# Last sixteen rows of the tenth K tile through Pool's DMA queue, w_mod in two loads (adaLN block with cached attention, decode step, one core)

## The chip, the cores and the metric

The kernel is one program on one core of one Trainium2 chip. A core has five engines with instruction streams of their own: TensorE (PE in the profile, its weight loads PEld), VectorE (DVE), ScalarE (ACT), GpSimd (POOL) and SyncE (SP), which here only issues transfers. Sixteen DMA engines move data between HBM and the core's SBUF, whose rows are 128 partitions; in this document they are called lanes, to keep them apart from the five. A transfer is issued by an instruction of SP, ACT or Pool, and each of these three has a queue of its own on the lanes. The metric is the device time of one execution in microseconds; the value for a kernel is the median of several runs.

## What is computed

One decode step of a transformer block for 8 sequences, all in float32: an adaptive layer norm from a condition `c`, attention of one new token over the last 2048 positions of a cache (32 query heads, 8 key and value heads, head size 128), a projection, a residual, a second adaptive layer norm and a feed-forward part with a squared ReLU.

```
mod = (silu(c) @ w_mod).reshape(8, 6, 1, 512)          # sa, ca, ga, sb, cb, gb
h = layernorm(x) * (1 + ca) + sa
q = (h @ wq) as 32 heads of 128
k, v = the last 2048 positions of k_cache, v_cache (8 heads, each used by 4 query heads)
o = softmax(q k^T / sqrt(128)) v
x = x + ga * (o @ wo)                                   # wo: 4096 x 512
h = layernorm(x) * (1 + cb) + sb
x = x + gb * (relu(h @ w1 + b1)^2 @ w2 + b2)            # 512 -> 1792 -> 512
```

Nearly all of the bytes are K and V: 8 heads x 8 sequences x 2048 positions x 128 numbers of 4 bytes is 67 MB each. With the weights the core reads 165 MB once, and each K and V number is used for four query heads only.

## The kernel before, in words

**Tiles.** K comes in 16 tiles, K0 to K15, and V in 16, each of 4 MB: for one key head, four of the eight sequences. A tile fills 128 partitions with 32 KB each. For K, partition 4p + u holds 64 consecutive positions of sequence u of the four, so the rows of the tile follow p, and within p the sequence u. The weights are w_mod (6 MB, 48 KB a partition), wq (8 MB), wo (four parts of 2 MB), w1 and w2.

**Slots.** SBUF holds four places of 4 MB ("big") and one of 2 MB ("small"), here all cut out of one tile called `home` (L80 to L85), so that w_mod, which takes a big and the small place side by side, is one transfer (L124), and wq, which takes two bigs, is one too (L128). The list `loads` (L144 to L149) fixes the order of all transfers: w_mod, wq, K0, K1, then alternately a K and a V tile with the parts of wo between them, and at the end the last V tiles, the last part of wo, w1 and w2. `pump` (L152) issues the next transfer of the list as soon as a place of its size is free, and `done` (L157) frees a place when its last reader has been written down. All of these are issued by SP and wait in SP's queue for the work that frees the place.

**Work.** DVE transposes each K tile in eight pieces (L190), PE makes the scores (L359), the softmax for a head runs over both its K tiles (L369 to L433, with ACT's exponentials), PE multiplies with V (L446) and projects with wo (L486). The order of the instructions on each engine is written out by hand in the loop over `s`; V work runs five steps (`PV_LAG`) behind. When the last wo product is done the second layer norm and the feed-forward part follow (L568 to L640). w2 is loaded in five pieces, the last two of one row group each (L136), and the multiplication with w2 (L630) follows the pieces as they land. The result leaves with one transfer (L640).

**The start.** The inputs `x` and `c` come, already laid out by the host, as `xc`: rows on four groups of 8 partitions (0 to 7, 32 to 39, 64 to 71, 96 to 103). ACT issues them in six transfers (L68): the first two carry x and c together, the rest one each. ACT's exponential for silu(c) (L201) waits for them, then follow DVE's statistics, PE's multiplication with w_mod (L278) and with wq (L304), and only then can scores begin.

**Pool** fills a few constants at the start, one more tile near the end (L502), and issues no transfer.

**Semaphores.** The transfers of SP and ACT share eight semaphores in rotation, in program order; one that takes a semaphore again waits for the transfer that had it before.

Of the kernel before, what the change touches and what calls it, by code (L numbers as in the profile page):

```python
# [8 lines left out]
F32 = mybir.dt.float32  # L9
# [4 lines left out]
EPS = 1e-5  # L14
BIG_SLOTS = 4
PV_LAG = 5


@with_exitstack
def tile_adaln_cached_attention_mlp(  # L20
# [14 lines left out]
    nc = tc.nc  # L35
    P = 128
    B, HKV, SK, DH = k_cache.shape
    D = wq.shape[0]
# [14 lines left out]
    consts = ctx.enter_context(tc.tile_pool(name="consts", bufs=1))  # L53
# [10 lines left out]
    nc.vector.memset(xc_in, 0.0)  # L64
    for q in range(D // P):
        b = slice(32 * q, 32 * q + B)
        for x, y in ((0, 2),) if q < 2 else ((0, 1), (1, 2)):
            nc.scalar.dma_start(xc_in[b, x:y], xc[b, x:y])  # L68

    ident = consts.tile([P, P], F32, name="ident")  # L70
# [6 lines left out]


    big = NJ * DH
    home = consts.tile([P, BIG_SLOTS * big + big // 2], F32, name="home")  # L80
    base = [2 * big, 0, big, 3 * big + big // 2]
    slots = {
        "big": [home[:, o : o + big] for o in base],
        "small": [home[:, 3 * big : 3 * big + big // 2]],
    }  # L85
    free = {size: list(range(len(ts))) for size, ts in slots.items()}
    held = {}

    def size_of(key):
        return "small" if key[0] in ("wo", "w1") or key == ("mod", 1) else "big"  # L90

    def load(key):
        kind, i = key
        held[key] = free[size_of(key)].pop(0)
        if kind in ("mod", "wq") and i == 0:
            return
        t = slots[size_of(key)][held[key]]
        if kind in "KV":

            hk, c = divmod(i, 2)  # L100
            v = k_cache[4 * c : 4 * c + 4, hk] if kind == "K" else v_cache[c::2, hk]
            v = v[:, SK - W :, :].rearrange("u (p j) d -> p u (j d)", j=NJ)
            cuts = (0, big // 2, big * 3 // 4, big) if key == ("V", 2 * HKV - 1) else (0, big)
            for x, y in zip(cuts, cuts[1:]):
                nc.sync.dma_start(t[:, x:y], v[..., x:y])
            return

        def rows(o, v):
            n = v.shape[1] * v.shape[2]
            nc.sync.dma_start(t[:, o : o + n].rearrange("p (a n) -> p a n", n=v.shape[2]), v)  # L110

        w1v = w1.rearrange("(p kc) n -> p kc n", p=P)

        def wo_rows(j):

            r = 2 * REP * DH
            return wo[j * r : (j + 1) * r, :].rearrange("(h p i) n -> p h (i n)", p=P, i=4)

        if kind == "wo":
            rows(0, wo_rows(i))  # L120
        elif kind == "mod":

            o = base[held["mod", 0]]
            nc.sync.dma_start(home[:, o : o + big + big // 2], w_mod.rearrange("(p kc) n -> p (kc n)", p=P))  # L124
        elif kind == "wq":

            o = base[held["wq", 0]]
            nc.sync.dma_start(home[:, o : o + 2 * big], wq.rearrange("(p k) n -> p (k n)", p=P))  # L128
        elif kind == "tail":
            rows(0, wo_rows(HKV // 2 - 1))  # L130
            rows(big // 2, w1v[:, 0:2])
        elif kind == "w1":
            rows(0, w1v[:, 2:4])
        else:
            v = w2.rearrange("(p c) n -> p c n", p=P)
            for lo, hi in ((0, 8), (8, 10), (10, 12), (12, 13), (13, 14)):  # L136
                rows(D * lo, v[:, lo:hi])
# [14 lines left out]
    def pump():  # L152
        while at[0] < len(loads) and free[size_of(loads[at[0]])]:
            load(loads[at[0]])
            at[0] += 1
# [86 lines left out]
    for k in (2, 3, 4):  # L242
        n = 1 << k
# [27 lines left out]
    for i, last in enumerate((16, 8)):  # L271
        at_ = 0
        while at_ < last:
            kc, m = divmod(16 * i + at_, 6)
            n = min(4 - m if m < 4 else 6 - m, last - at_)
# [233 lines left out]

    for s in range(N + PV_LAG + 1):  # L510
        g, i = divmod(s, C)
        q, h = divmod(s, 2)
        v = s - PV_LAG
        soft = 1 <= g <= HKV
# [122 lines left out]
    y = work.tile([P, P], F32, name="y", tag="one_y", bufs=1)  # L637
# [39 lines left out]
```

## Time and profile before

| | |
|---|---|
| median of 3 runs | 394.15 us (393.83 to 394.23) |
| profiled execution | 393.95 us |
| its span, first to last instruction | 392.2 us |
| PE busy | 251.7 us (64%) |
| DVE busy | 219.6 us (56%) |
| ACT busy | 46.1 us (12%) |
| Pool busy | 1.3 us (0%) |
| read from HBM | 164.67 MB, 420 GB/s over the span |
| SP's queue (q1) | 7424 packets, 98.2% of the lanes' time |

The span runs from the first to the last instruction; the profiled execution's own time is 1.75 us more. A busy share of the lanes is the time that packets took, over 16 lanes. A packet on SP's queue is one row of a transfer in one partition, 32 KB for a K or V tile, or the 4 bytes with which a lane tells that its share of a transfer has landed. In the chain of work that ended last, "DMA home<-..." is time in which that chain waited for a transfer to land. The queue called "instruction" carries the programs of the engines themselves, fetched in blocks while the kernel runs.

### The profile page before, as it was taken

What the parts mean: (1) busy time and instruction counts of PE and PEld (TensorE: products, weight loads), DVE (VectorE), ACT (ScalarE), POOL (GpSimd) and SP (SyncE); (2) the same over time, 40 slices, a digit from 0 to 9 for tenths busy, and PEclk for the clock granted to TensorE, in tenths of its full rate; (3) what the DMA queues carried; (4) which work ended last, traced back from release to release, by engine and by line L of the source; (5) the groups of instructions that cost most, each with busy time, mean ns of one, the idle gap of its engine ahead of it and who ended that gap; (6) DMA issues with size and microseconds to landing.
All of it is one profiled execution on the core that took longest, in us unless ns stands there. A gap on an engine that the chain in (4) does not pass through costs nothing.

```text
span 392.2 us, 4671 instructions
## 1 busy us (share of the span) xinstructions
PE 251.7 (64%) x2006; PEld 77.0 (20%) x2006; DVE 219.6 (56%) x315; ACT 46.1 (12%) x89; POOL 1.3 (0%) x8
## 2 busy tenths in 40 slices
PE   0006859779328873897384828882874838896796
PEld 0002211012102221222121202220221202233333
DVE  1006479998057735783582817881676358755231
ACT  0012021131003100310031002010111003004010
POOL 0000000000000000000000000000000000000000
PEclk9999989999959995999598797998697969998999
DMA  8999999999999999999999999999999999999994
GB/s 327 444 442 431 434 431 431 428 426 404 450 428 431 426 431 431 423 436 445 429 423 434 434 429 428 428 429 428 409 445 431 433 431 434 428 418 419 426 421 177
DMA packets 7557, 165.04 MB, mean 421 GB/s; under 512 B 824, under 2 KB 1008, under 8 KB 1520
## 3 DMA queue, kind: packets, MB, share of 16 engines
q1 hardware_dynamic: 7424, 164.70, 98.2%
q8 instruction: 16, 0.26, 0.3%
q10 hardware_dynamic: 112, 0.04, 0.0%
q14 instruction: 5, 0.04, 0.0%
HBM read 164.67 MB, written 0.07 MB: 420 GB/s over the span
## 4 chain that ended last, share of the span: by engine, by line
DMA 61%; DVE 20%; PE 14%; issue 3%; ACT 1%; ACTq 0%; POOL 0%; DVEq 0%; POOLq 0%; SPq 0%
DMA home<-in_A_k_cache_dram 44%; DVE kT L190 12%; PE s_ps L359 7%; DMA xc_in<-in_xc_dram 6%; DMA home<-in_B_w_dram 6%; DMA home<-in_A_v_cache_dram 5%; PE o_ps L446 2%; PE m_ps L304 2%; DVE pT L425 2%; PE p_ps L390 1%; DVE pr L418 1%; DVE qbd L322 1%; DVE o_sb L464 1%; DVE mx L373 0%; DVE qst L268 0%
## 5 line engine op out<-in xcount | busy, mean ns | idle before, releaser
L190 DVE STREAM_TRANSPOSE kT<-home 128x1024 f32<-128x1024 f32 x128 | 151.2, 1219 | 83.8 <-DMA home<-in_A_k_cache_dram 79.6
L359 PE MATMUL s_ps<-kT,qst 128*32 128x512 f32 x512 | 129.2, 1076 | 20.5 <-DVE kT L190 19.5
L446 PE MATMUL o_ps<-home,pT 128*32 128x256 f32 x1024 | 70.0, 397 | 10.6 <-DVE pT L425 9.7
L446 PEld LDWEIGHTS o_ps<-home,pT 128*32 128x32 f32 x1024 | 33.9, 117 | 101.4 <-issue 62.4
L375 PE MATMUL m_ps<-ident,mx 128*1 128x128 f32 x16 | 4.3, 365 | 58.8 <-DVE mx L373 58.8
L359 PEld LDWEIGHTS s_ps<-kT,qst 128*32 128x32 f32 x512 | 14.4, 115 | 40.4 <-DVE kT L190 32.0
L224 PE MATMUL m_ps<-xsum,sel 128*128 128x1 f32 x2 | 0.6, 362 | 32.5 <-DVE xsum L222 32.5
L425 DVE STREAM_TRANSPOSE pT<-pr 128x2048 f32<-128x2048 f32 x8 | 18.2, 2274 | 1.0 <-ACT pr L408 1.0
L408 ACT ACTIVATE pr<-pr,own 128x512 f32<-128x512 f32 x16 | 17.8, 1220 | 0.3
L402 ACT ACTIVATE pr<-p_ps,nm 128x512 f32<-128x512 f32 x8 | 5.5, 688 | 96.8 <-DVE nm L399 96.8
L347 ACT COPY qst<-q_ps 32x128 f32<-32x128 f32 x32 | 8.2, 256 | 70.2 <-PE q_ps L336 70.0
L369 ACT COPY ss<-s_ps 128x512 f32<-128x512 f32 x8 | 4.7, 585 | 98.9 <-issue 69.9
L202 DVE TENSOR_SCALAR e_sb<-e_sb 128x128 f32<-128x128 f32 x1 | 0.2, 226 | 27.2 <-ACT e_sb L201 27.2
L375 PEld LDWEIGHTS m_ps<-ident,mx 128*1 128x1 f32 x16 | 0.7, 81 | 64.0 <-DVE mx L373 64.0
L390 PE MATMUL p_ps<-ss,perm 128*128 128x512 f32 x16 | 12.1, 844 | 0.0
L399 DVE TENSOR_SCALAR nm<-m_ps 128x1 f32<-128x1 f32 x8 | 1.3, 159 | 16.8 <-PE m_ps L395 16.8
L418 DVE TENSOR_SCALAR pr<-pr,own 128x512 f32<-128x512 f32 x16 | 9.2, 656 | 0.8 <-ACT pr L402 0.8
L486 PE MATMUL wo_ps<-home,oT 128*32 128x512 f32 x64 | 8.3, 600 | 1.8 <-DMA home<-in_A_wo_dram 1.8
L463 DVE TENSOR_SCALAR o_sb<-o_ps,bit 128x128 f32<-128x128 f32 x16 | 4.9, 306 | 6.1 <-PE o_ps L446 6.1
L429 PE MATMUL m_ps<-zs,tsel 128*128 128x8 f32 x16 | 2.9, 252 | 8.1 <-DVE zs L420 8.1
L304 PE MATMUL m_ps<-home,h1T 128*32 128x512 f32 x64 | 7.1, 594 | 1.5 <-DVE add L294 1.5
L278 PE MATMUL m_ps<-home,cT 128*32 128x512 f32 (+1 forms) x64 | 7.6, 642 | 0.0
(118 smaller groups left out, 115.5 us busy)
## 6 DMA issues: line engine op xcount, KB each, us to landing
home<-in_A_k_cache_dram SPq DMA_DIRECT2D x16, 4096.0 KB, 23.9
home<-in_A_v_cache_dram SPq DMA_DIRECT2D x15, 4096.0 KB, 20.3
home<-in_A_wo_dram SPq DMA_DIRECT2D x4, 2048.0 KB, 25.7
home<-in_w_mod_dram SPq DMA_DIRECT2D x1, 6144.0 KB, 17.4
home<-in_B_w_dram SPq DMA_DIRECT2D x2, 1792.0 KB, 28.5
home<-in_A_v_cache_dram SPq DMA_DIRECT2D x1, 2048.0 KB
home<-in_A_v_cache_dram SPq DMA_DIRECT2D x2, 1024.0 KB
home<-in_B_w_dram SPq DMA_DIRECT2D x1, 2048.0 KB
```

What stands on the lines that cost most here:

```text
L190: nc.vector.transpose(KTS[q, j][:, rows], k[:, rows, 32 * j : 32 * j + 32])
L278: nc.tensor.matmul(pms[m // 4][32 * q : 32 * q + 32, m % 4 * P : (m % 4 + n) * P].rearrange("p (m n) -> p m n", n=P), cT[:, kc, :], wv[:, ...
L304: nc.tensor.matmul(pqs[r][32 * g : 32 * g + 32, :], hT[:, kc, :], w[:, 4 * r + g, :], start=(kc == 0), stop=(kc == NQ - 1),)
L347: nc.scalar.copy(own[b, :, :, i, 0], pq[b, :P].rearrange("p (c m t) -> p c m t", c=2, t=REP))
L359: nc.tensor.matmul(s_ps[0][32 * g : 32 * g + 32, :], qst[hk % 2][:, P * (4 * c + u) + 32 * j :][:, :32], kT[:, u], start=(c == 0 and j == ...
L390: nc.tensor.matmul(sp, perm, SS_.pop(hk), start=True, stop=True)
L402: nc.scalar.activation(pr.rearrange("p j x -> p (j x)"), SS_.pop(hk), AF.Exp, bias=nm, scale=SCALE, accum_out=z)
L408: nc.scalar.mul(X_[hk][..., w], pr, own[:, w : w + 1])
L418: nc.vector.tensor_scalar(X_[hk][..., w], pr, own[:, w : w + 1], None, op0=ALU.mult)
L425: nc.vector.transpose(PT_[hk].rearrange("p e j r -> p j e r"), X_.pop(hk).rearrange("p j x w -> p j (x w)"))
L446: nc.tensor.matmul(O_[n][32 * g : 32 * g + 32, : 2 * DH], PT_[hk][:, e, j : j + 2].rearrange("p j r -> p (j r)"), vt[:, j : j + 2, :].rear ...
L486: nc.tensor.matmul(wo_ps[32 * i : 32 * i + 32, :], oT[hk % 2][:, i, :], w[:, 4 * (hk % 2) + i, :], start=(hk == 0), stop=(hk == HKV - 1),)
```

## The change

The sixteen rows p = 16 to 31 of sequence u = 3 of the tile K9 (partitions 67, 71, ... 127) are loaded by Pool's queue, in six transfers of 3, 2, 4, 3, 2 and 2 rows. Between them stand five transfers of 4, 6, 4, 5 and 6 single numbers of b1 into a tile `step` that nothing reads. The table `WALK` lists all eleven, with 1 for rows and 0 for unread numbers. The other 112 rows of K9 come in four transfers of SP's queue, one for each sequence u: 32, 32, 32 and 16 rows, each going to every fourth partition.

With it, `home` loses the 2 MB place, which becomes a tile `small` of its own, and the big places change order. w_mod comes in two transfers, 32 KB a partition to a big place and 16 KB a partition to `small`. `xc` comes in eight transfers instead of six, each with x or c alone. The first and the third part of wo come in two transfers each. In all, SP and ACT issue eight transfers more: two for xc, one for w_mod, two for wo and three for K9. No computing instruction is added, removed or moved on any engine.

```diff
--- before.py
+++ after.py
@@ -14,6 +14,7 @@
 EPS = 1e-5
 BIG_SLOTS = 4
 PV_LAG = 5
+WALK = ((3, 1), (4, 0), (2, 1), (6, 0), (4, 1), (4, 0), (3, 1), (5, 0), (2, 1), (6, 0), (2, 1))
 
 
 @with_exitstack
@@ -64,7 +65,7 @@
     nc.vector.memset(xc_in, 0.0)
     for q in range(D // P):
         b = slice(32 * q, 32 * q + B)
-        for x, y in ((0, 2),) if q < 2 else ((0, 1), (1, 2)):
+        for x, y in ((0, 1), (1, 2)):
             nc.scalar.dma_start(xc_in[b, x:y], xc[b, x:y])
 
     ident = consts.tile([P, P], F32, name="ident")
@@ -77,12 +78,13 @@
 
 
     big = NJ * DH
-    home = consts.tile([P, BIG_SLOTS * big + big // 2], F32, name="home")
-    base = [2 * big, 0, big, 3 * big + big // 2]
+    home = consts.tile([P, BIG_SLOTS * big], F32, name="home")
+    base = [3 * big, 0, big, 2 * big]
     slots = {
         "big": [home[:, o : o + big] for o in base],
-        "small": [home[:, 3 * big : 3 * big + big // 2]],
+        "small": [consts.tile([P, big // 2], F32, name="small")],
     }
+    step = consts.tile([8, len(WALK)], F32, name="step")
     free = {size: list(range(len(ts))) for size, ts in slots.items()}
     held = {}
 
@@ -92,7 +94,7 @@
     def load(key):
         kind, i = key
         held[key] = free[size_of(key)].pop(0)
-        if kind in ("mod", "wq") and i == 0:
+        if key == ("wq", 0):
             return
         t = slots[size_of(key)][held[key]]
         if kind in "KV":
@@ -100,6 +102,20 @@
             hk, c = divmod(i, 2)
             v = k_cache[4 * c : 4 * c + 4, hk] if kind == "K" else v_cache[c::2, hk]
             v = v[:, SK - W :, :].rearrange("u (p j) d -> p u (j d)", j=NJ)
+            if key == ("K", 9):
+
+                d = t.rearrange("(p u) n -> u p n", u=4)
+                for u in range(4):
+                    n = 32 if u < 3 else 16
+                    nc.sync.dma_start(d[u][:n], v[:n, u])
+                for j, (m, real) in enumerate(WALK):
+                    if real:
+                        nc.gpsimd.dma_start(d[3][n : n + m], v[n : n + m, 3])
+                        n += m
+                    else:
+                        nc.gpsimd.dma_start(step[:m, j : j + 1], b1[:m].rearrange("(a n) -> a n", n=1))
+                assert n == 32
+                return
             cuts = (0, big // 2, big * 3 // 4, big) if key == ("V", 2 * HKV - 1) else (0, big)
             for x, y in zip(cuts, cuts[1:]):
                 nc.sync.dma_start(t[:, x:y], v[..., x:y])
@@ -117,11 +133,13 @@
             return wo[j * r : (j + 1) * r, :].rearrange("(h p i) n -> p h (i n)", p=P, i=4)
 
         if kind == "wo":
-            rows(0, wo_rows(i))
+            cuts = (0, 2) if i == 1 else (0, 1, 2)
+            for x, y in zip(cuts, cuts[1:]):
+                rows(4 * D * x, wo_rows(i)[:, x:y])
         elif kind == "mod":
 
-            o = base[held["mod", 0]]
-            nc.sync.dma_start(home[:, o : o + big + big // 2], w_mod.rearrange("(p kc) n -> p (kc n)", p=P))
+            v = w_mod.rearrange("(p kc) n -> p (kc n)", p=P)
+            nc.sync.dma_start(t, v[:, big:] if i else v[:, :big])
         elif kind == "wq":
 
             o = base[held["wq", 0]]
```

## The prediction

> **What bounds the kernel now.** I read the page's header and DMA part first, then the chain of waits, then stretches of time with the lanes' busy share, and last the waits of single engines.
>
> ```profile
> span 392.2 us, 4671 instructions
> ...
> DMA  8999999999999999999999999999999999999994
> ...
> q1 hardware_dynamic: 7424, 164.70, 98.2%
> q8 instruction: 16, 0.26, 0.3%
> ```
>
> ```profile
> 20.00:380.00 360.00, 242.92 (x1874) 72.39 (x1876) 216.11 (x300) 46.01 (x89) 0.47 (x1) 0.90 1.00 428
> 385.00:385.50 0.50, 0.50 (x20) 0.50 (x24) 0.00 (x0) 0.00 (x0) 0.00 (x0) 1.00 0.70 270
> 385.50:386.00 0.50, 0.50 (x29) 0.50 (x22) 0.00 (x0) 0.00 (x0) 0.00 (x0) 1.00 0.62 250
> 386.00:386.50 0.50, 0.50 (x28) 0.50 (x22) 0.00 (x0) 0.00 (x0) 0.00 (x0) 1.00 0.48 193
> 386.50:387.00 0.50, 0.50 (x28) 0.50 (x24) 0.00 (x0) 0.00 (x0) 0.00 (x0) 1.00 0.49 188
> 387.00:387.50 0.50, 0.49 (x19) 0.22 (x12) 0.00 (x0) 0.00 (x0) 0.00 (x0) 1.00 0.52 201
> 387.50:388.00 0.50, 0.50 (x16) 0.26 (x14) 0.00 (x0) 0.00 (x0) 0.00 (x0) 1.00 0.36 135
> 388.00:388.50 0.50, 0.45 (x12) 0.16 (x8) 0.00 (x0) 0.00 (x0) 0.00 (x0) 1.00 0.01 4
> ```
>
> ```profile
> 344.99 21.49 DMA home<-in_A_v_cache_dram
> 366.54 22.08 DMA home<-in_B_w_dram
> 388.62 0.04 issue
> 388.67 0.47 PE m_ps L630 x8
> 389.16 0.30 DVE y L638
> 389.48 0.29 DVE y L639
> ```
>
> The last two columns of a stretch are the lanes' busy share and GB/s. From 20 to 380 us the share is 1.00: no lane runs dry, and 428 GB/s over 16 lanes is 26.75 GB/s each, so a 32 KB row takes 1.22 us and a 4 MB tile 9.8 us. The chain ends on the landing of w2's last rows; after it come only eight matmuls, two DVE steps and the output. So the time is the end of the latest lane plus a fixed tail. The lanes do not end together: the share falls to 0.5 by 386 and stays there until 388. Summed over the six stretches from 385 to 388, what is missing to 1.00 is 1.4 us; that, with 0.1 to 0.2 us after 388, is the most that a perfect balance of the lanes could save.
>
> The packet records (start, length, queue, size) show which lanes. On a lane a packet starts 3 to 5 ns before the last one ends, so the records can be strung into sixteen lanes of 464 packets of SP's queue each:
>
> ```
> end of last w2 row, us                            program blocks that the lane fetched before
> 384.95 384.95 385.05 385.16 385.17                none
> 385.38 385.69 385.99                              one
> 387.67 387.71 387.77 387.86 387.88 387.93 388.08  two of 16 KB
> 388.16                                            three of 8 KB
> ```
>
> A 16 KB block takes 1.06 us and makes the row behind it 0.47 us longer: 1.5 us, twice on the same seven lanes. This imbalance is what moving rows can work on.
>
> **The change: the small edits.**
>
> ```profile
> 1.18 0.42 SPq L128 DMA_DIRECT2D home<-in_A_wq_dram  x1
> ...
> 27.88 1.28 ACT L201 ACT_TABLE_LOAD   x1 [27.88 <-DMA xc_in<-in_xc_dram]
> ...
> 34.42 7.57 PE L278 MATMUL m_ps<-home,cT 128*32 128x512 f32 x64
> ```
>
> ```profile
> home<-in_A_wq_dram SPq DMA_DIRECT2D x1, 36.4
> ```
>
> ```profile
> 43.48 7.08 PE m_ps L304 x64
> ...
> 54.29 2.43 DVE kT L190 x3
> ```
>
> xc lands at 27.9 because each of its packets takes turns with a 48 or 64 KB row of SP's queue. With w_mod's rows of 32 and 16 KB the sixteen turns of eight xc transfers (one for the row, one for its completion) fit into w_mod's time, so xc lands near 18 us (estimate). L278 moves with it; L304 can start when wq lands, 1.2 + 36.4 = 37.6 instead of 43.5, and the transposes up to 6 us sooner. It is worth nothing: the share is 1.00, so the first K tiles are no bound of the end. The other way, w_mod's second transfer waits for the first xc transfer (it reuses the next semaphore). The first eight rows last until about 1.8 + 8 x 1.22 = 11.6 us; xc's first must land before about 10, and with shorter rows to wait for it should at 7. If not, the lanes idle for the difference; I take 0, bound 1.2 us, one row. Splitting wo, and all other added transfers, costs completion packets: 8 + 11 transfers at 9 ns are 0.17 us a lane at most; I take 0.1. Since eight transfers of SP and ACT are added, the rotation of eight semaphores stands as before from the last wo on.
>
> **The change: issuing K9.**
>
> ```profile
> 180.13 0.54 SPq L105 DMA_DIRECT2D home<-in_A_k_cache_dram  x1
> 200.66 0.53 SPq L105 DMA_DIRECT2D home<-in_A_v_cache_dram  x1
> 206.62 0.54 SPq L105 DMA_DIRECT2D home<-in_A_k_cache_dram  x1
> 223.09 0.54 SPq L105 DMA_DIRECT2D home<-in_A_v_cache_dram  x1
> 225.27 0.54 SPq L105 DMA_DIRECT2D home<-in_A_k_cache_dram  x1
> ```
>
> ```profile
> 214.49 6.88 DVE L190 STREAM_TRANSPOSE kT<-home 128x1024 f32<-128x1024 f32 x6 [7.27 <-DMA home<-in_A_k_cache_dram]
> ```
>
> ```profile
> POOL pr L502 <- DVE pT L425: 357.1, 1, 357.1
> ```
>
> ```profile
> out_dram<-y SPq DMA_DIRECT2D x1, 64.0 KB, 1.5
> ```
>
> K9 is issued at 180.1 and read at 214.5. SP's three more issues cost 3 x 0.54 = 1.6 us; behind them stands V7, which goes out at 200.7 anyway. Pool has nothing to do until 358 us. Its issue is not in the trace: between 0.54 us as on SP and 0.54 + 1.5 with a whole landing after each, eleven take 6 to 22 us, inside the 34 us. If that cover were gone, DVE would start K9 late and K11 (225.3) be issued late; ahead of K11 in the queue are then V7, K10 and V8, so some 18 us are left before a lane runs dry. I take 0.
>
> **The change: which lane carries which row.** As WALK reads, with a cursor that starts at lane 0 and goes on by one lane per row or number, three lanes get 10 rows of K9 (0, 7, 8), three get 9 (1, 2, 15), one 8 and nine 7, instead of 8 each. If each row kept its 1.22 us and the +2 lanes were ones that end at 385.0, they would end at 387.4 and the late ones at 386.9: 0.7 us less than 388.1.
>
> But the rows also change partitions. In every load of before that has 128 partitions, all rows take the same time, whatever the tile. The few small loads show what a foreign write does. Four rows of b1 and b2 go to partitions 0 to 3 on four lanes, and xc's last two transfers to 96 to 103 on eight:
>
> ```
> lane        what it carries   rows of SP's queue, ns (usual 311 / 2418)
> one of b's  own w rows        422, 335, 361 right after b1 and b2
> one         own wq rows       2467 and 2512, at xc's last two
> another     own wq rows       2447 and 2501, at the same
> ```
>
> Only these three lanes are slowed, by 199, 142 and 112 ns. The foreign bytes, at 26.75 B/ns, are 3 x (1792 + 512) = 258 ns for the first and 2 x 2048 = 153 ns for each of the others, so the lane that owns a stripe of partitions loses some 0.8 of the time of foreign bytes. The four earlier xc transfers slowed nobody, so it isn't a law.
>
> The Trainium skill has the rule ("SBUF — State Buffer", section on door 1, the DMA port swizzle): sixteen ports, chosen by bits of the partition number, and a transfer's rate goes by how many ports its partitions reach. It agrees with the three slowed lanes; by it two lanes on one port get half each.
>
> These small loads deal one row to one lane whatever the partition, so K9's loads by u will hardly hit each lane's own stripe, and neither will Pool's. Price per SP row: between 0 (1.22 us stays) and a doubling, +1.22. I take the half, since lanes are out of step by up to a row: 7 x 0.61 = 4.3 us. A Pool row runs beside a stripe's owner all the time: 0.8 x 1.22 = 0.98, three are 2.9 us. Sum for a +2 lane: 385.0 + 2.4 + 4.3 + 2.9 + 0.1 = 394.7, against 388.1 before: +6.6. A late lane gets 388.1 - 1.2 + 4.3 and about one Pool row of others on its stripe, 1.0: 392.2, which does not decide. The profiled execution's 393.95 becomes 400.5, 0.2 below what the median's 394.15 would give. Bounds: -0.7 with no sharing, and 2.4 + 8.5 + 3.7 + 0.1 = 14.7 on 385.0, so 399.7 and +11.6, with every row doubled.
>
> **Rivals.**
> Balance works: foreign rows cost nothing at 32 KB, as with the four xc transfers that slowed nobody. 393.4. Against it are the three slowed lanes.
>
> Wrong lanes: no sharing, but the cursor isn't at lane 0, or a +2 lane is one of the eight late ones. Then 388.1 + 2.4 = 390.5, time 396.4. It decides as soon as one late lane gets one row more. Nothing in the trace tells a lane's number to Pool. The Trainium skill ("DMA: Bandwidth & Descriptors", on why a semaphore rises by 16) gives the cursor, consecutive engines in round robin, but also tells of direct copies from Pool that are dealt over sixteen engines from engine 0 on. By that exception lane 0 would get six Pool rows, 13 in all, five more than before: 385.0 + 6.1 = 391.1, time 397.0. No run here shows either.
>
> Nothing moves: a stripe's eight K9 rows are its own bound, whoever writes them, and a late lane's stripe ends as late as before. 394.2, within 0.2%. For it: a row's constant 1.22 us could be the stripe's as well as the lane's.
>
> **How the numbers follow.** Sharing 0.60 (400.5, own range 396.5 to 405.7); wrong lanes 0.13; balance 0.17; nothing 0.10. Two tenths of a per cent, 0.8 us, is about what can be told here. Balance at -0.7 lies on that edge: 0.11 faster, 0.06 same. Same 0.16, slower 0.73. The range from 393.4 to 405.7 takes in the rivals.
>
> **What would show it.** Sharing: K9's transposes start later than 214.5, the busy share stays near 1 in K9's time while GB/s falls by a fifth or more, and the tail below full share after 385 gets longer than 3 us. Balance: the share stays near 1 until 387 and the end is sooner. Wrong lanes: GB/s stays, the tail at low share gets longer. The early start: L201 near 18 us. I am wrong if GB/s between 180 and 225 us is as before.

## The result

| | before | after |
|---|---|---|
| median | 393.97 us (393.83 to 394.23) | 408.94 us (407.51 to 409.55) |
| profiled execution | 393.95 us | 407.51 us |
| its span | 392.2 us | 405.7 us |

The ratio is 1.0373, 95% interval 1.0361 to 1.0385: slower by 15 us. The prediction was 400.5 us with a range up to 405.7; the sign was right and the time lies above the range.

The page of the kernel after: header, the two rows of DMA in forty slices (busy tenths and GB/s), and the queues with packets, MB and share.

```profile
span 405.7 us, 4709 instructions
...
DMA  8999999999999999999999999999999999999992
GB/s 353 477 414 405 418 423 452 417 425 441 423 427 443 422 424 448 420 425 368 307 345 288 439 425 427 410 415 417 428 446 420 448 423 412 428 412 420 429 413 97
...
q1 hardware_dynamic: 7632, 164.17, 97.0%
q0 software_dynamic: 352, 0.53, 0.6%
```

The lanes are as busy as before in every slice but the last, yet in slices 19 to 22 they move 288 to 368 GB/s. The same by stretches of the kernel after; the last two columns are the lanes' busy share and GB/s.

```profile
180.00:190.00 10.00, 3.74 (x41) 1.48 (x40) 0.37 (x1) 0.59 (x1) 4.22 (x8) 0.94 1.01 377
190.00:200.00 10.00, 5.40 (x29) 1.45 (x29) 5.81 (x6) 0.00 (x0) 1.56 (x3) 0.54 1.06 350
200.00:210.00 10.00, 7.94 (x62) 2.32 (x62) 9.29 (x14) 3.02 (x4) 0.00 (x0) 1.00 1.01 319
210.00:220.00 10.00, 2.67 (x16) 0.46 (x12) 0.00 (x0) 0.00 (x0) 0.00 (x0) 0.81 1.04 307
220.00:230.00 10.00, 2.88 (x22) 1.20 (x14) 0.89 (x1) 1.03 (x4) 0.00 (x0) 0.67 0.94 383
385.00:390.00 5.00, 4.46 (x30) 1.52 (x26) 2.05 (x9) 0.79 (x3) 0.00 (x0) 1.00 1.01 431
390.00:395.00 5.00, 4.91 (x37) 1.43 (x36) 0.69 (x3) 0.34 (x2) 0.00 (x0) 1.00 0.97 403
395.00:400.00 5.00, 4.88 (x72) 2.99 (x72) 1.47 (x4) 0.00 (x0) 0.00 (x0) 1.00 0.53 208
400.00:402.00 2.00, 1.84 (x55) 1.04 (x44) 0.00 (x0) 0.00 (x0) 0.00 (x0) 1.00 0.13 43
```

Against the 428 GB/s of before, the five stretches from 180 to 230 lack 404 GB/s x 10 us = 4.0 MB, or 9.4 us on the average lane. That is two thirds of the loss. The share stays at 0.97 up to 395, is 0.53 from 395 to 400 and 0.13 after (0.13 x 16, two lanes). By the packet records the first lane is through with w2 at 396.1 and the last at 401.6, where before it was 385.0 and 388.2. So every lane is late, the first by 11.1 us and the last by 13.4, and the lanes end 5.5 us apart instead of 3.2. Where the first lane loses what it is late beyond the 9.4 was not followed.

The chain of work that ended last, kernel after (start, length, what):

```profile
182.21 46.59 DMA home<-in_A_k_cache_dram
...
229.11 2.38 DVE kT L208 x2
...
358.40 21.37 DMA home<-in_A_v_cache_dram
379.84 22.18 DMA home<-in_B_w_dram
402.02 0.04 issue
402.06 0.47 PE m_ps L648 x8
```

K9 is read at 229.1, 14.6 us later than before (214.49), and w2's last rows land at 402.0 in place of 388.6. Behind them stands the same tail.

### The profile page after: what moved, and what is told of

Same layout as the page of the kernel before. It is cut to its first block, busy times and chain, and to the rows that moved or that the text cites. A ratio compares the mean times of both kernels' runs of the same rounds, so it can differ in the third digit from the quotient of the medians.

```text
span 405.7 us, 4709 instructions
## 1 busy us (share of the span) xinstructions
PE 255.9 (63%) x2006; PEld 78.3 (19%) x2006; DVE 219.6 (54%) x315; ACT 46.2 (11%) x89; POOL 7.1 (2%) x19
## 4 chain that ended last, share of the span: by engine, by line
DMA 75%; PE 11%; DVE 11%; issue 1%; SPq 0%; POOL 0%; DVEq 0%; POOLq 0%
DMA home<-in_A_k_cache_dram 55%; DVE kT L208 9%; DMA home<-in_A_wq_dram 7%; PE s_ps L377 7%; DMA home<-in_B_w_dram 5%; DMA home<-in_A_v_cache_dram 5%; PE m_ps L322 2%; DMA xc_in<-in_xc_dram 2%; PE o_ps L464 2%; DVE qbd L340 1%; DVE o_sb L482 1%; SPq L110 0%; DVE o_sb L481 0%; PE m_ps L337 0%; PE m_ps L648 0%
## 5 line engine op out<-in xcount | busy, mean ns | idle before, releaser
L464 PE MATMUL o_ps<-home,pT 128*32 128x256 f32 x1024 | 71.0, 400 | 10.0 <-DVE pT L443 9.7
L322 PE MATMUL m_ps<-home,h1T 128*32 128x512 f32 x64 | 9.0, 723 | 6.8 <-DMA home<-in_A_wq_dram 6.8
L504 PE MATMUL wo_ps<-small,oT 128*32 128x512 f32 x48 | 7.2, 677 | 7.3 <-DMA small<-in_A_wo_dram 7.3
L340 DVE COPY qbd<-m_ps 32x128 f32<-32x128 f32 x8 | 3.0, 372 | 15.0 <-PE m_ps L337 14.8
```

Of the source, the lines that this page charges most:

```text
L322: nc.tensor.matmul(pqs[r][32 * g : 32 * g + 32, :], hT[:, kc, :], w[:, 4 * r + g, :], start=(kc == 0), stop=(kc == NQ - 1),)
L340: nc.vector.tensor_copy(qbd[b, 4 * r : 4 * r + 4, j].rearrange("p g (b t) -> p t g b", t=REP), pT_[b].rearrange("p (t g b) -> p t g b", t= ...
L464: nc.tensor.matmul(O_[n][32 * g : 32 * g + 32, : 2 * DH], PT_[hk][:, e, j : j + 2].rearrange("p j r -> p (j r)"), vt[:, j : j + 2, :].rear ...
L504: nc.tensor.matmul(wo_ps[32 * i : 32 * i + 32, :], oT[hk % 2][:, i, :], w[:, 4 * (hk % 2) + i, :], start=(hk == 0), stop=(hk == HKV - 1),)
```

## The experiments

All of them are the kernel after with its block for K9 changed; the small edits (xc, w_mod, wo) stay. A diff that shows only added lines has them in place of the block's two loops. The kernel before was run beside each group: medians 393.85, 393.80, 393.86 and 393.90 us. Where an expectation speaks of the sharing theory, it is the one of the prediction.

### The small edits, and the four loads of SP's queue

`one_load`: K9 by one transfer.

```diff
-            if key == ("K", 9):
-                ...
-                return
```

> The kernel after with K9 as one load of SP's queue again; the other edits (xc in eight transfers, w_mod in two, two of the wo tiles in two) stay. Sharing theory (a row written outside the partitions that its lane writes in a 128-partition load takes time from the lane that owns them, and loses as much itself): nothing foreign is left beside xc, so 394.0 us, within 0.8 of the kernel before. Rival A, the other edits carry the loss: about 409, as the kernel after. Rival B, Pool's queue alone costs the time: 394 too. GB/s from 180 to 230 us as before, 406 to 446.

Measured 394.17, ratio 1.0018 (1.0000 to 1.0035). The small edits are worth nothing that can be told; the loss is in K9's block.

`four_by_u`: four full loads, one per sequence, no Pool.

```diff
                 for u in range(4):
-                    n = 32 if u < 3 else 16
-                    nc.sync.dma_start(d[u][:n], v[:n, u])
-                for j, (m, real) in enumerate(WALK):
-                    ...
+                    nc.sync.dma_start(d[u], v[:, u])
```

> K9 in four loads of SP's queue, one per u, each to the 32 partitions u, u+4, ...; nothing from Pool. Every lane carries eight rows, as before the change. Sharing theory: the rows fall on half of the stripes at a time, two lanes on each, so a row takes 2.4 us in place of 1.22 and all lanes end 8 x 1.22 = 9.8 us later: 403.8 (402 to 406). Half price, as my prediction took it: 8 x 0.61 = 4.9, 398.9. Rival B, the loss is Pool's queue or the unequal number of rows: 394.2. Rival C, the number of transfers: the same as the cut by columns.

Measured 393.97, ratio 1.0010 (0.9996 to 1.0024): a clear miss of both sharing prices. In the stretch where the kernel after falls to 307 to 350 GB/s, this one shows (columns as above):

```profile
190.00:200.00 10.00, 6.99 (x42) 2.16 (x46) 7.70 (x9) 1.67 (x3) 0.00 (x0) 0.70 0.94 399
200.00:210.00 10.00, 7.94 (x71) 2.28 (x67) 7.39 (x12) 1.35 (x2) 0.00 (x0) 1.00 1.06 449
210.00:220.00 10.00, 4.06 (x38) 1.36 (x34) 5.47 (x5) 1.02 (x4) 0.00 (x0) 0.66 0.98 423
```

Its rows of 32 KB took 1213 to 1224 ns from the 10th to the 90th in a hundred of each 4 us from 176 to 232, as in the kernel before (1213 to 1225). So a load to every fourth of the 128 partitions disturbs nobody. That its rows are dealt so that each lane keeps to its own partitions is the simplest reading; the lanes' numbers are not in the records.

`four_by_columns`, the control for the number of transfers:

```diff
+                for y in range(4):
+                    s = slice(y * big // 4, (y + 1) * big // 4)
+                    nc.sync.dma_start(t[:, s], v[..., s])
```

> K9 in four loads of SP's queue that each go to all 128 partitions, a quarter of the columns each: four transfers, but every row on the lane that writes those partitions anyway. Sharing theory: 394.2. Rival C, four transfers in the place of one cost the time: as the four loads by u, 399 to 404. Rival B: 394.2.

Measured 394.14, ratio 1.0006 (0.9997 to 1.0015). The number of transfers costs nothing.

`two_halves`, two loads by halves of the partitions:

```diff
+                for h in range(2):
+                    nc.sync.dma_start(t[64 * h : 64 * h + 64], v[16 * h : 16 * h + 16])
```

> K9 in two loads of SP's queue, partitions 0 to 63 and 64 to 127, four rows per lane each; the rows are read from HBM in the same order as in one load. Sharing theory: each load reaches half of the stripes and two lanes write each, so 8 rows x 1.22 = 9.8 us more: 403.8 (402 to 406). Rival D, the order of the addresses in HBM (a load by u reads one stretch of 1 MB, the whole tile four stretches in turn): 394.2. Rival C, number of transfers: less than the four loads by columns cost, 394 to 395.

Measured 406.36, ratio 1.0316 (1.0303 to 1.0330), just above the range that sharing gave. Same bytes, same order in HBM, two transfers and no Pool:

```profile
200.00:210.00 10.00, 7.93 (x64) 2.15 (x60) 7.89 (x12) 1.83 (x2) 0.00 (x0) 1.00 1.16 289
210.00:220.00 10.00, 1.52 (x22) 0.69 (x14) 0.00 (x0) 1.02 (x4) 0.00 (x0) 0.72 0.98 208
```

208 GB/s is half of 428. Half of the partitions take half of the rate, and the lanes look fully busy with it: their rows of 32 KB took 2.45 to 2.54 us at the median of each 4 us from 204 to 220. The order of addresses in HBM is no cause.

`no_pool_rows`: SP's four loads as in the kernel after, Pool's eleven left out.

```diff
-                for j, (m, real) in enumerate(WALK):
-                    ...
```

> The kernel after without Pool's eleven loads: SP's four loads stay (seven rows per lane), and sixteen rows of K9 are not loaded, so that the scores of those rows come from what stood in the slot. Sharing theory: one row less per lane, 1.2 us, and seven rows at the doubled price, 7 x 1.22 = 8.5: 394 - 1.2 + 8.5 = 401.3 (399 to 403); what is left to the kernel after, 7.6 us, is then the price of Pool's sixteen rows. Half price: 394 - 1.2 + 4.3 = 397.1. Rival B, Pool's queue carries the loss: 392.8.

Measured 395.40, ratio 1.0041 (1.0026 to 1.0056). One row less per lane would make it 392.6; so SP's load of 16 rows costs 2.8 us by itself and the three loads of 32 nothing. Those sixteen rows go to partitions 3, 7, ... 63, so they lie in one half only, as each load of `two_halves` does, while the loads of 32 rows reach both. The other 13.5 us of the loss come with Pool's sixteen rows.

### Pool's queue

`pool_whole`, K9 by one load of Pool's queue:

```diff
+                nc.gpsimd.dma_start(t, v)
```

> K9 by one load of Pool's queue to all 128 partitions; nothing of K9 on SP's queue. Sharing theory: if Pool deals the 128 rows over the lanes as SP does, each writes its own partitions and nothing is shared: 394.2 (393.4 to 395), with Pool's rows at 1.22 us. Rival B, rows of Pool's queue are slow by themselves (1.92 to 2.36 us in the kernel after, so 0.7 to 1.1 too much): eight per lane, 400 to 403.

Measured 394.25, ratio 1.0011 (1.0002 to 1.0021); Pool's 128 rows took 1213 to 1221 ns up to the 90th in a hundred. Pool's queue is not slow by itself.

`pool_by_eight_0` and `pool_by_eight_1`, sixteen loads of eight rows, in two orders:

```diff
+                d = t.rearrange("(a c u) n -> a u c n", c=8, u=4)
+                for s in range(2):
+                    for u in range(4):
+                        for h in (0, 1):          # (1, 0) in the twin
+                            a = 2 * h + s
+                            nc.gpsimd.dma_start(d[a, u], v[8 * a : 8 * a + 8, u])
```

> K9 by sixteen loads of Pool's queue, eight rows each: in turn a load to partitions 4c+u (+32s) and one to 64+4c+u (+32s), c from 0 to 7. If Pool deals one row per lane with a cursor that starts at lane 0 and goes on by eight, each row is on the lane that owns its partitions. Sharing theory with that cursor: 394.2 (393.4 to 395). Sharing theory without it: as the next kernel, later by 5 to 10 us. Rival B: 400 to 403 in both.

> As the kernel with sixteen Pool loads, but of each two the load to partitions from 64 on goes first: each row is then on the lane eight further than the one that owns its partitions. Same number of loads, rows, bytes and lanes. Sharing theory with the cursor at lane 0: each row shares with the owner's row of SP's queue, eight rows on each lane, at 0.8 to 1.22 us each lost on both sides at once: 400 to 404. Rival B and every theory that counts queues, transfers or rows per lane: the same time as its twin.

Measured 422.03, ratio 1.0699 (1.0669 to 1.0728), and 423.38, ratio 1.0730 (1.0684 to 1.0775). Both are alike and far above every number in the expectations. The packet records of Pool's rows, load by load, tell why:

```
lengths of Pool's eight rows, ns   partitions 0 to 63 first   partitions 64 to 127 first
first load                         1214 to 1221               1912 to 2425
second                             1898 to 2327               1213 to 1225
third                              1213 to 1344               1886 to 2401
fourth                             1906 to 2347               1213 to 1221
fifth                              1213 to 1222               1856 to 2332
```

In these five, loads to the lower half run near the undisturbed 1.21 and loads to the upper half don't, in either order. From the seventh or eighth load on, the loads follow each other by some 3 us, and rows of the lower half are long too (up to 2347). A cursor that goes on by eight would have made one kernel fast throughout and the other slow throughout. So each load of eight rows goes to the same eight lanes, those that own partitions 0 to 63. The landings say the same, one per lane and transfer: the part of wo that SP issued ahead of V7 landed on eight lanes at 205.3 to 209.4 us and on the other eight at 234.6 to 240.3 in the first kernel, at 207.6 to 210.7 and 236.9 to 242.1 in the second. With a cursor all sixteen would be level.

`no_unread`, the kernel after without the unread loads:

```diff
-                for j, (m, real) in enumerate(WALK):
-                    ...
+                n = 16
+                for m in (3, 2, 4, 3, 2, 2):
+                    nc.gpsimd.dma_start(d[3][n : n + m], v[n : n + m, 3])
+                    n += m
```

> The kernel after without Pool's five loads of unread numbers; Pool's six loads of 3, 2, 4, 3, 2 and 2 rows stay. Theory L (each load of Pool starts at lane 0, whatever went before, so that lanes 0 and 1 carry six Pool rows each): nothing moves, 408.5 (407.5 to 409.5), fewer completions being worth 0.3 us at most. Theory C (a cursor goes on from load to load, as my prediction had it): the sixteen rows fall on sixteen lanes one after the other, one each, so 398 to 400.

Measured 408.11, ratio 1.0359 (1.0342 to 1.0376), as theory L says, 8 to 10 us from theory C. The unread numbers steer nothing. The packet counts of Pool's queue say the same; one line each from the pages of the kernel after (eleven loads), `no_unread` (six), `sixteen_in_one` (one load of 16 rows) and `pool_whole` (one load of 128):

```profile
q0 software_dynamic: 352, 0.53, 0.6%
```

```profile
q0 software_dynamic: 192, 0.52, 0.5%
```

```profile
q0 software_dynamic: 32, 0.52, 0.6%
```

```profile
q0 software_dynamic: 144, 4.19, 2.5%
```

352 is 11 x 32, 192 is 6 x 32 and 144 is 16 x (8 + 1). Every load, of 2 rows or of 16, puts two packets on each of sixteen lanes: a share, which for a lane without a row is 4 bytes, and a completion. A load that takes all sixteen lanes has no place to go on from. Where the rows themselves went, the landings of V7 show, the tile behind K9 in SP's queue (us, in order of time, one per lane):

```
before            221.5 221.7 221.9 222.0 222.0 222.2 222.3 222.7 223.3 223.3 223.3 223.4 223.4 223.5 223.6 224.2
kernel after      229.9 230.2 230.8 230.9 231.1 231.5 231.5 231.5 231.9 231.9 232.0 232.3 233.8 234.9 238.2 238.5
no_unread         230.0 230.2 230.5 230.7 230.8 231.5 231.8 231.8 232.1 232.1 232.2 232.3 233.4 234.9 238.3 239.1
```

With every load starting at the same lane, called lane 0 here, lanes 0 and 1 have thirteen rows of K9, lane 2 ten, lane 3 eight and the other twelve seven: at 1.22 us a row they should be 7.3, 7.3, 3.7 and 1.2 us behind the twelve. In the kernel after they are 7.0, 6.7, 3.4 and 2.3 behind the middle of the twelve, 231.5. The cursor would have left seven lanes behind the other nine in the kernel after and none in `no_unread`.

`sixteen_in_one`, Pool's sixteen rows in one load:

```diff
-                for j, (m, real) in enumerate(WALK):
-                    ...
+                nc.gpsimd.dma_start(d[3][16:], v[16:, 3])
```

> The kernel after with its sixteen Pool rows in a single Pool load, no unread numbers. One row per lane by either theory, each outside its lane's partitions, as SP's load of sixteen rows, which cost 395.4 - (394.0 - 1.2) = 2.6 us in the kernel without Pool's rows. So 395.4 + 1.2 + 1 to 2.6 = 397.6 to 399.2. Theory L: the 10 us to the kernel after are then the price of six rows on each of two lanes. Sharing alone, wherever the rows are: as the kernel after, 406 to 409.

Measured 398.00, ratio 1.0106 (1.0091 to 1.0121), as both theories of the lanes expected, and far from sharing alone. The same sixteen rows in the same partitions from the same queue cost 2.6 us here and 13.5 in the kernel after; 1.2 of each is the row that every lane has more than in `no_pool_rows`.

`pool_own_half` and `pool_foreign_half`, eight loads of eight rows to one half; the other half of K9 is not loaded:

```diff
+                d = t.rearrange("(a c u) n -> a u c n", c=8, u=4)
+                for s in range(2):
+                    for u in range(4):
+                        a = 0 + s                 # 2 + s in the twin
+                        nc.gpsimd.dma_start(d[a, u], v[8 * a : 8 * a + 8, u])
```

> K9 by eight loads of Pool's queue of eight rows each, to partitions 4c+u and 32+4c+u, c from 0 to 7, u from 0 to 3; partitions 64 to 127 of K9 are not loaded and keep what stood there. Theory L: lanes 0 to 7 carry these 64 rows, in their own partitions, eight rows each as with one load; the other lanes carry eight less. 394.0 (393.2 to 395), Pool's rows at 1.22 us. Theory C: every second load falls on lanes 8 to 15 and shares: later, 396 to 400.

> The twin: the same eight loads of eight rows to partitions 64 to 127; partitions 0 to 63 of K9 are not loaded. Theory L: the same lanes 0 to 7 carry eight rows each, now in partitions that lanes 8 to 15 write at the same time. A Pool row takes 2.1 us in place of 1.22: 8 x 0.9 = 7 us more than the twin, 401 (399 to 404); lanes 8 to 15 have the 9.8 us to spare that they do not load. Theory C: the same time as the twin, since half of the loads is foreign in both.

Measured 394.37, ratio 1.0005 (0.9984 to 1.0026), and 408.68, ratio 1.0377 (1.0358 to 1.0396). Loads, rows per load, bytes and queue are the same, and in both the part of wo ahead of V7 lands on eight lanes late, 9 and 13 us behind the other eight (middle to middle), so eight lanes carry them in both; by the pair above they are the same eight. The rows come from other places in HBM, but these same rows took 1.21 in `pool_whole`. So the partitions make 14.3 us. All 64 rows of the first took 1213 to 1222 ns, those of the second 1900 to 2473. The first and then the second kernel in the same stretch:

```profile
190.00:200.00 10.00, 4.40 (x24) 1.34 (x28) 5.80 (x6) 0.00 (x0) 0.00 (x0) 0.55 0.96 410
```

```profile
190.00:200.00 10.00, 2.24 (x10) 0.49 (x10) 5.25 (x6) 0.00 (x0) 0.00 (x0) 0.50 1.01 288
```

But 14.3 is twice the 7 us expected from Pool's rows alone, so something beside the Pool rows is slowed too.

`two_of_eight` and `sixteen_of_one`, Pool's sixteen rows in two loads of eight and in sixteen of one:

```diff
-                for j, (m, real) in enumerate(WALK):
-                    ...
+                for n in (16, 24):
+                    nc.gpsimd.dma_start(d[3][n : n + 8], v[n : n + 8, 3])
```

```diff
-                for j, (m, real) in enumerate(WALK):
-                    ...
+                for n in range(16, 32):
+                    nc.gpsimd.dma_start(d[3][n : n + 1], v[n : n + 1, 3])
```

> The kernel after with its sixteen Pool rows in two Pool loads of eight rows. Theory L (each load starts at lane 0): lanes 0 to 7 carry two of them each. One such row costs 398.0 - 395.4 = 2.6 us, so 395.4 + 2 x 2.6 = 400.6 (399.5 to 402). Theory C (cursor): one row per lane, 398.0.

> The kernel after with its sixteen Pool rows in sixteen Pool loads of one row. Theory L: all sixteen on lane 0, 395.4 + 16 x 2.25 to 2.6 = 431 to 437 (2.25 from six rows on one lane in the kernel after, 2.6 from one row on each). Theory C: 398. If a load of a single row is dealt in another way (its 32 KB cut over the lanes): 396 to 397.

Measured 400.89, ratio 1.0185 (1.0164 to 1.0206), as theory L expected; and 402.80, ratio 1.0231 (1.0214 to 1.0248), a miss of all three numbers. The records have 256 packets of 2048 bytes on Pool's queue: a row of its own is cut over all sixteen lanes, as the third possibility had it, but it still costs 7.4 us, 0.46 per load, of which 1.2 us in all are the rows themselves.

### What one load outside its lanes' partitions costs

The first Pool load of the kernel after has three rows. All rows of 32 KB that the sixteen lanes carry around it, in order of start, lengths in ns:

```
start 184.65 to 185.44, SP's   1384 1454 1554 1665 1780 1765 1838 1952 1933 2062 2078 2086 2219
start 185.19 to 185.60, Pool's 1955 2015 2362
start 186.03 to 187.96, SP's   2298 2245 2148 2076 1936 1919 1946 1774 1758 1748 1698 1635 1621 1766 1487 1346
start 188.33 to 189.30, SP's   1213 to 1245, all sixteen
```

Three rows are foreign, so at most three owners and three carriers should suffer. Instead all sixteen lanes do: no row that runs while Pool's three are in flight, 185.2 to 188.0, has its 1.21. Added up over 1214 ns a row, the load costs 20.7 us of lane time, 1.29 us on each lane. In the same way I summed for each kernel what all packets of SP's and Pool's queues from 176 to 250 us took beyond the undisturbed packet of their size (5.9 us in the kernel before, taken off) and divided by 16. The next column is 1.22 us per row of K9 that the fullest lane has beyond eight.

| kernel | foreign Pool loads | lost per lane, us | fullest lane | sum | time less before |
|---|---|---|---|---|---|
| `no_pool_rows` | none | 2.6 | -1.2 | 1.4 | 1.6 |
| `sixteen_in_one` | 1 of 16 rows | 4.0 | 0 | 4.0 | 4.1 |
| `two_of_eight` | 2 of 8 | 6.0 | 1.2 | 7.2 | 7.0 |
| `sixteen_of_one` | 16 of 1, cut | 8.1 | 0 | 8.1 | 8.9 |
| `no_unread` | 6 of 2 to 4 | 10.0 | 6.1 | 16.1 | 14.3 |
| after | 6 of 2 to 4 | 9.6 | 6.1 | 15.7 | 15.0 |
| `pool_own_half` | none | 0.2 | 0 | 0.2 | 0.5 |
| `pool_foreign_half` | 8 of 8 | 13.9 | 0 | 13.9 | 14.8 |
| `pool_by_eight_0` | 8 of 8 (8 own) | 16.8 | 9.8 | 26.6 | 28.2 |
| `pool_by_eight_1` | 8 of 8 (8 own) | 17.6 | 9.8 | 27.4 | 29.6 |
| `two_halves` | SP's two of 64 | 11.0 | 0 | 11.0 | 12.5 |

Nothing in the table is fitted, and the sums meet the times within 2.2 us. Where the sum is above the time, the fullest lanes may be such as end early; their ends differ by up to 3 us in the kernel before.

The lost time goes by loads and hardly by rows: above `no_pool_rows`, a foreign load of sixteen rows costs each lane 1.4 us, of eight rows 1.7, and six loads of 2 to 4 rows 7.0 to 7.4, or 1.2 each. It goes better still by time: sum up, for each kernel, how long at least one foreign row of Pool's was in flight. That is 3.7 us with one load of sixteen rows, 15.6 with the sixteen cut rows, 19.5 in the kernel after and 31 to 42 with eight loads of eight rows. In all eight kernels with such rows, each lane lost 0.35 to 0.45 of this time, beyond the 2.6 of SP's load of 16 rows where that is there. So a load of two rows costs nearly as much as one of sixteen because it is in flight nearly as long. This reading came after the runs, and no kernel was made to test it alone. Why a write that shares a lane's partitions holds up lanes that have nothing to do with it stays open.

## Why the prediction was wrong

**The bound, the small edits, the issuing, the completions: right.** The lanes' share stays near 1 and w2's last rows still end the time. xc's first reader runs near 18 us, as said, and brings nothing (`one_load`). On Pool and ACT, kernel after:

```profile
16.30 1.28 ACT L219 ACT_TABLE_LOAD   x1 [16.30 <-DMA xc_in<-in_xc_dram]
18.48 0.31 ACT L219 ACTIVATE e_sb<-xc_in 128x128 f32<-128x128 f32 x1 [0.90 <-DMA xc_in<-in_xc_dram]
```

```profile
180.67 0.65 POOL L113 DMA_DIRECT2D home<-in_A_k_cache_dram  x1 [179.22 <-DVE kT L208]
...
190.03 0.52 POOL L113 DMA_DIRECT2D home<-in_A_k_cache_dram  x1 [5.14 <-DMA home<-in_A_k_cache_dram]
191.46 0.52 POOL L116 DMA_DIRECT2D step<-in_B_b_dram  x1 [0.90 <-DMA step<-in_B_b_dram]
196.04 0.52 POOL L113 DMA_DIRECT2D home<-in_A_k_cache_dram  x1 [4.07 <-DMA home<-in_A_k_cache_dram]
```

Pool's eleven issues take 15.9 us, three of them waiting for earlier landings: inside the 6 to 22 us of the prediction.

**Which lane carries which row: the step that failed.** The prediction took "a cursor that starts at lane 0 and goes on by one lane per row or number", and so gave each of three lanes ten rows of K9, three of these from Pool. Every Pool load of 2 to 16 rows starts at lane 0 (`no_unread`, the kernels with eight rows, the packet counts, the landings of V7). So lanes 0 and 1 have a row from each of the six loads, thirteen rows of K9 in all, lane 2 three and lane 3 one, and the unread loads move nothing. That is five rows, 6.1 us, more than before in place of two, 2.4: the 2.4 of the sum was the wrong placement's. The rival "wrong lanes" had this very placement, from the exception in the Trainium skill ("DMA: Bandwidth & Descriptors", on why a semaphore rises by 16: some direct copies take all sixteen engines, from engine 0 on). Here every load of 2 to 16 rows was such a copy, and no run shows the cursor.

**The price of foreign writes: wrong in its parts.** Three terms stood in the sum.

- SP's rows, "I take the half", 4.3 us: six of the seven cost nothing (`four_by_u`). The load of 16 rows, which was not told apart from the others, costs 2.6 to 2.8 us alone. That the loads of 32 rows, which reach both halves of the partitions, are harmless was not considered.
- Pool's rows, "0.8 x 1.22 = 0.98, three are 2.9 us": one load costs 1.2 us on every lane, and there are six, 7.0 us.
- The late lanes, "392.2, which does not decide": the price falls on all sixteen lanes, and the share of 0.97 from 390 to 395 us shows them still at work. The premise was that only a stripe's owner is slowed, as the b1, b2 and xc rows of the kernel before had it. (The first of these three lanes is 185 ns over its usual rows by the lengths shown, not 199; 0.8 of the foreign bytes' time, 440 of 564 ns, still comes out.) The Trainium skill ("SBUF — State Buffer", section on door 1) has a transfer's rate go by the number of ports that its partitions reach, eight of sixteen for either half of them. The half rate is there: 208 GB/s in `two_halves`. But rows to partitions that nobody else writes are slowed as well (all 32 rows around the first Pool load), and that the three slowed lanes of before had not shown.

With the measured terms the fullest lane gets 6.1 + 2.6 + 7.0 = 15.7 us, against 15.0 measured.

**The range.** "Wrong lanes" and "sharing" stood as rivals with one condition each, "no sharing" in the first. Both happened at once. The upper bound doubled every row of a lane with ten rows; it had no case for thirteen, nor for rows of other tiles. The signs given for sharing all came: K9's transposes at 229.1, GB/s lower by a tenth to over a quarter at full share (383 to 307 against 428), a tail of 7 us instead of 3.

**What could be won.** The most that balance could save was 1.4 to 1.6 us, and a single foreign load costs 1.2 us on every lane. No run came out below the kernel before by more than can be told; the best, `four_by_u`, was 393.97.

## What to carry to other kernels

Before rows are moved between DMA lanes, find out where a queue puts a small transfer: count the packets of the queue per transfer, see how far apart the lanes land the next transfer, and time the same small transfer to two sets of partitions. A kernel bound by its lanes should load in transfers that spread over all partitions, by columns, whole or by every fourth partition here; transfers of 64 rows to one half of the partitions ran at half the rate, and a small one outside its lanes' partitions held up all the others too. A busy share of 1.00 does not tell a lane at full rate from one that is held up (1.04 at 307 GB/s here), so read GB/s beside it.

## What the runs showed of the hardware that was not expected

- A load of a few rows outside its lanes' partitions slows all sixteen lanes while it is in flight, 2.8 us for the first three rows of the kernel after: 1.2 to 1.7 us lost on each for one load, whether of 2 to 4 rows or of sixteen.
- A Pool load of one row of 32 KB is cut into sixteen pieces of 2048 bytes. The pieces take 84 to 140 ns (nine in ten), but each such load costs the kernel 0.46 us.
- Four SP loads of 32 rows, each to every fourth partition, cost nothing, while two of 64 rows to halves cost 12.5 us.
- A Pool load of all 128 partitions runs at the same 1.21 us per row as SP's, beside SP's own rows.
